# A state-space scan and a dilated local attention on one core: q·k products laid out by head dimension, and the scan as a tree in PSUM

## The chip, the core and the metric

The kernel runs on one core of one Trainium2 chip. The time is the device time in microseconds (us) of one execution; of several executions the median is given. The engines of a core work beside each other and meet through semaphores: TensorE (PE, matrix products into PSUM; its weight loads are a row of their own, PEld), VectorE (DVE), ScalarE (ACT), GpSimd (POOL) and SyncE (SP), whose queue issues most of the transfers. The trace comes from one profiled execution.

## The reference

Two independent heads work on inputs of 2048 positions and 448 channels, and their outputs stand side by side in 896 columns.

Head A is a diagonal state-space model with 448 complex states. With `Lam_bar = exp(dt*Lam)` and `B_bar = ((Lam_bar-1)/Lam)*B` it computes, position after position,

```
h = Lam_bar * h + B_bar @ x[t]
y[t] = 2 * Re(C @ h) + Dskip * x[t]
```

Head B is attention with 16 heads of 28 dimensions. `q, k, v = x @ wqkv`; a position attends to itself and to the positions 2, 4, ..., 14 before it (8 taps, `w`), those before the start being masked; softmax over the taps; the weighted sum of v goes through `wo`. Inputs and output are bf16.

## The kernel before, in words

The 2048 positions are cut into 128 chunks of 16. A chunk is a partition wherever positions lie on partitions, and `j` (0 to 15) is the place in the chunk, so that a tile `[128, 16, 448]` holds a whole head's input.

**Head B.** `prep` (L197) transposes x for each j on PE (L213), copies it to SBUF (`xT`, ACT, L216) and multiplies it with Wk (`_proj_unit`, L189), chunks on the output's partitions. DVE copies k to `kd` (L219), ACT q to `qd` (L232), both as `[128 chunks, j, dim, head]`. Positions from the chunk before (a halo of 14) come by DMA within SBUF (`_halo`). `qk` (L255) takes, for each block of 8 j (`b` = 1, then 0) and each tap w, one product of 3584 elements a partition (L265), adds the upper half of the 28 dimensions to the lower (L267) and again to 7 (L270), and PE adds those 7 into PSUM with an identity as weights (L276). ACT copies the logits out (L282), POOL masks (L288). `softmax` (L299) takes maximum and sum by halving over the taps on DVE. `pv` (L328) multiplies attention weights and v and accumulates on DVE (L348, L351, L352) in three parts of 8, 6 and 2 j, with two partial sums; per j PE transposes and adds these (`pt_o`, L364), ACT copies (`oT`, L369), PE multiplies with `wo` (L374), ACT copies (`yb`, L379), SP stores (L382).

**Head A.** `setup` derives, from the parameters, the powers of Lam_bar as small arrays and from those matrices of 128x128 for each of 7 tiles (`m`) of 64 complex states (real parts on 64 partitions, imaginary on 64): Gdiag, Lmat, Mmat on POOL (L585, L615), Pmat on DVE (L615). `level1` (L682) runs over j: B_bar times x into PSUM (L712, 128 columns), plus Lmat times the state of j-1 (L720), copied out by ACT (L724) and stored to DRAM (`hs`). `level2` scans the 128 chunk ends in 7 doubling steps (L749, L754). `outputs` (L783) loads each j's states again (L793), adds the carry from the chunk before with identity and power matrices (L803, L805), copies (L809), and makes y (L821, L826), which ACT copies (L831) and SP stores (L837).

**Order.** Nothing runs in the order of the source. Every step is a `Unit` of `Planner` with an engine, an estimated cost, dependences, a priority and perhaps a buffer to acquire or release (PSUM tags mm 4, pt 2, lg 2 banks). `Planner.run` simulates the engines by the estimated costs, always starts the unit that can start first (ties by priority), and emits the instructions in that order. On the chip each engine keeps this order and waits where something isn't ready.

Of the kernel before, what the change touches and what calls it, by code (L numbers as in the profile page):

```python
# [10 lines left out]
ALU = mybir.AluOpType  # L11
f32 = mybir.dt.float32
# [16 lines left out]
NST = 7  # L29
PAD = 64  # L30
MA = 4
JB = 8
NB = T // JB
BH = JB * H
# [8 lines left out]
def act(n):  # L43
    return n / 1200.0 + 0.16


def vec(n):
    return n / 960.0 + 0.15


def vec2(n):
    return n / 1920.0 + 0.15
# [6 lines left out]
class Unit:  # L59
    __slots__ = ("eng", "cost", "fn", "deps", "prio", "acq", "rel", "lat", "end", "seq")  # L60


class Planner:

# [6 lines left out]
    def add(self, eng, cost, fn, deps=(), prio=0.0, acq=None, rel=None, lat=0.08):  # L71
        u = Unit()
        u.eng, u.cost, u.fn, u.prio, u.acq, u.rel, u.lat = eng, cost, fn, prio, acq, rel, lat
        u.deps = [d for d in deps if d is not None]
        u.end, u.seq = None, len(self.units)
        self.units.append(u)
        return u

    def run(self):
        left = list(self.units)  # L80
        clock = {}
        order = []
        while left:
            best = None
            for eng in {u.eng for u in left}:
                now = clock.get(eng, 0.0)
                pick = None
                for u in left:
                    if u.eng != eng or any(d.end is None for d in u.deps):
                        continue  # L90
                    if u.acq and not self.free[u.acq]:
                        continue
                    t = max([now] + [d.end - (d.lat if d.eng == eng != "SP" else 0.0) for d in u.deps])
                    if u.acq:
                        t = max(t, min(self.free[u.acq]))
                    key = (t, u.prio, u.seq)
                    if pick is None or key < pick[0]:
                        pick = (key, u)
                if pick and (best is None or pick[0][0] < best[0][0]):
                    best = pick  # L100
            assert best, "no unit can start"
            (t, _, _), u = best
            if u.acq:
                self.free[u.acq].remove(min(self.free[u.acq]))
            clock[u.eng] = t + u.cost
            u.end = t + u.cost + u.lat
            if u.rel:
                self.free[u.rel].append(u.end)
            left.remove(u)
            order.append((t, u))  # L110
        self.order = order
        for _, u in order:
            u.fn()


def _make_identity(nc, ident):
    n = ident.shape[0]
    nc.gpsimd.memset(ident, 0.0)
    nc.gpsimd.affine_select(
        out=ident, in_=ident, compare_op=ALU.not_equal, fill=1.0, base=0,  # L120
        pattern=[[-1, n]], channel_multiplier=1,
    )


class PartB:
    JG = (3, 2, 1, 0)
    PV = ((1, 8, 16, "xin"), (0, 0, 6, "qd"), (0, 6, 8, "lg"))

    def __init__(self, tc, B_x, B_wqkv, B_wo, out_b, ident, pool, psum, plan):
        self.tc, self.nc = tc, tc.nc  # L130
        self.B_x, self.B_wqkv, self.B_wo, self.out_b = B_x, B_wqkv, B_wo, out_b
        self.ident, self.pool, self.psum, self.plan = ident, pool, psum, plan

    def loads(self):
        nc, pool, P = self.nc, self.pool, self.plan
        self.x_sb = pool.tile([NCH, T, D], bf16, name="xb_sb", tag="xin")
        xv = self.B_x[0].rearrange("(p j) d -> p j d", j=T)
        self.wn = pool.tile([KP, KT, 3, H, DH], bf16, name="wqkv_nat", tag="wp")
# [3 lines left out]
        def xload(g):  # L142
            nc.sync.dma_start(self.x_sb[:, 4 * g:4 * g + 4], xv[:, 4 * g:4 * g + 4])

        def wload(w):
            nc.sync.dma_start(self.wn[:, :, w].rearrange("p k h d -> p k (h d)"), wv[w])
        for i, g in enumerate(self.JG):
            self.u_x[g] = P.add("SP", dma(458752), lambda g=g: xload(g), lat=2.5)
            w = {0: 1, 2: 0, 3: 2}.get(i)
            if w is not None:  # L150
                self.u_w[w] = P.add("SP", dma(401408), lambda w=w: wload(w), lat=2.5)
# [11 lines left out]
    def alloc(self):  # L163
        nc, pool, V = self.nc, self.pool, self.nc.vector
        self.qd = pool.tile([NCH, T, DH, H], bf16, name="qd", tag="qd")
        self.kd = pool.tile([NCH, TJ, DH, H], bf16, name="kd", tag="kd")
        self.vx = pool.tile([NCH, TJ * DH * H], bf16, name="vd", tag="vd")
        self.vd = self.vx[:].rearrange("p (j d h) -> p j d h", d=DH, h=H)
        self.xT = self.vx[0:KP, 0:T * KT * NCH].rearrange("p (g k j c) -> p g k j c", g=4, k=KT, j=4)
        self.zsrc = pool.tile([1, DH * H], bf16, name="zsrc")  # L170
        V.memset(self.zsrc[:], 0.0)

    def _zero(self, t_):
        self.nc.sync.dma_start(t_[0:1, 0:HALO].rearrange("o j d h -> o j (d h)"),
                               self.zsrc[:].unsqueeze(1).to_broadcast([1, HALO, DH * H]))

    def _halo(self, t_, i0, i1):
        nc = self.nc
        nc.sync.dma_start(t_[1:113, i0:i1], t_[0:112, i0 + T:i1 + T])
        nc.sync.dma_start(t_[113:128, i0:i1], t_[112:127, i0 + T:i1 + T])  # L180

    def _proj_unit(self, j, which, prio, deps, evict, eng, extra=()):
        nc, P = self.nc, self.plan
        box = {}

        def mm():
            ps = self.psum.tile([NCH, H, DH], f32, name="qkv_ps", tag="mm")
            for k in range(KT):
                nc.tensor.matmul(ps[:].rearrange("p h d -> p (h d)"), lhsT=self.xT[:, j // 4, k, j % 4, :],  # L189
                                 rhs=self.wn[:, k, which].rearrange("p h d -> p (h d)"),  # L190
                                 start=(k == 0), stop=(k == KT - 1))
            box["ps"] = ps[:].rearrange("p h d -> p d h")
        u = P.add("PE", pe(4, 448), mm, [self.u_xe[j], self.u_w[which], *deps], prio, acq="mm")
        e = P.add(eng, act(448), lambda: evict(box["ps"]), [u, *extra], prio, rel="mm")
        return u, e

    def prep(self):  # L197
        nc, P, V = self.nc, self.plan, self.nc.vector
        self.u_xe, self.u_k, self.u_kh, self.u_q = {}, {}, {}, {}
        self.u_proj = []  # L200
        self.lg, self.u_lg, self.u_d, self.u_attn = {}, {}, {}, {}
        self.attn = None
        P.add("SP", 0.1, lambda: self._zero(self.kd), prio=0)
        for g in self.JG:
            if g == 1:
                self.q_proj(1, 0)
            for j in range(4 * g + 3, 4 * g - 1, -1):
                box = {}
# [724 lines left out]
```

## Time and profile before

| | us |
|---|---|
| median of three executions | 183.8 |
| lowest, highest | 182.88, 183.84 |
| span of the profiled execution, first to last instruction | 180.6 |
| PE, DVE, ACT, POOL busy | 161.8, 157.2, 114.5, 26.8 |
| first DVE operation on data, end of the last | 8.2, 172.7 |
| first matmul | 4.73 |

The page gives no time for the profiled execution but its span; what lies around it is the rest of an execution's time, which is here taken from the median, 183.8 − 180.6 = 3.2 us. In a row of groups the columns are: line, engine, operation, output and inputs by name, shapes, how many, then busy us, mean ns of one, and idle time before them with what ended it. In an order of time: start, duration, engine, line, operation. In the chain: start, duration, what. A matmul's duration holds a latency that the next one overlaps, so PE's pace is read from the chain. In the stretch view: stretch, its length, busy time of PE, PEld, DVE, ACT, POOL, then the granted clock (1.00 is full), DMA's share, GB/s.

### The profile page before, as it was taken

How to read it: one execution, taken by the hardware profiler on the slowest of the kernel's cores; microseconds unless marked ns; L12 is line 12 of the kernel's file. 1: busy time of each engine (PE TensorE's matmuls, PEld its weight loads, DVE VectorE, ACT ScalarE, POOL GpSimd, SP SyncE). 2: the span in 40 equal slices, each digit the busy share in tenths (PEclk: the TensorE clock that was granted, in tenths of full speed). 3: DMA queues.
4: the chain of work that ended last, by engine and by line, in shares of the span. 5: the costliest groups of instructions: out<-in, count | busy, mean ns of one | idle time of the engine just before them, and what ended most of it. 6: DMA issues, size and time to landing. Idle time of an engine off the chain costs nothing.

```text
span 180.6 us, 4508 instructions
## 1 busy us (share of the span) xinstructions
PE 161.8 (90%) x1840; PEld 121.1 (67%) x1840; DVE 157.2 (87%) x175; ACT 114.5 (63%) x227; POOL 26.8 (15%) x39
## 2 busy tenths in 40 slices
PE   0889999098999999998999998989999899999992
PEld 0556567054689999964999984566777667667760
DVE  0187999999999999999999987999999999999920
ACT  2358767205788735699574358986666578756863
POOL 2000599996000000001000010000000000000000
PEclk9999999969999999999999999999999999999999
DMA  6999633637771112211454223155544323351322
GB/s 168 342 269 210 151 101 98 206 83 244 129 129 61 33 58 92 88 59 31 126 160 126 89 67 95 51 157 162 169 155 152 105 73 104 104 156 54 95 85 76
DMA packets 24643, 22.20 MB, mean 123 GB/s; under 512 B 9243, under 2 KB 23093, under 8 KB 24623
## 3 DMA queue, kind: packets, MB, share of 16 engines
q1 hardware_dynamic: 24552, 21.91, 43.8%
q8 instruction: 14, 0.23, 0.6%
q14 instruction: 6, 0.05, 0.1%
q10 hardware_dynamic: 71, 0.01, 0.0%
HBM read 11.36 MB, written 7.34 MB: 104 GB/s over the span
## 4 chain that ended last, share of the span: by engine, by line
DVE 44%; PE 38%; issue 11%; DMA 2%; ACT 2%; POOL 0%; POOLq 0%; DVEq 0%; ACTq 0%
DVE prod L265 11%; PE qkv_ps L189 9%; DVE prod L267 7%; PE wo_ps L374 7%; DVE pv_tmp L351 7%; DVE acc L352 6%; PE y_ps L826 5%; DVE s L270 5%; PE pt_o L364 4%; DMA xb_sb<-in_B_x_dram 2%; PE l1A L712 2%; PE pt_x L213 2%; DVE kd L219 2%; PE l1B L712 1%; DVE logits L310 1%
## 5 line engine op out<-in xcount | busy, mean ns | idle before, releaser
L189 PE MATMUL qkv_ps<-wqkv_nat,vd 112*128 112x448 bf16 x192 | 43.5, 369 | 1.0 <-ACT vd L216 0.5
L265 DVE TENSOR_TENSOR prod<-qd,kd 128x3584 bf16<-128x3584 bf16 x16 | 33.5, 2096 | 0.4
L189 PEld LDWEIGHTS <-vd 112*128 112x128 bf16 x192 | 18.4, 101 | 16.0 <-issue 3.0
L712 PEld LDWEIGHTS <-Bcat 112*128 112x128 bf16 x448 | 26.3, 98 | 0.0
L352 DVE TENSOR_TENSOR acc<-acc,pv_tmp 128x3584 bf16<-128x3584 bf16 (+2 forms) x18 | 25.3, 1403 | 0.6
L351 DVE TENSOR_TENSOR pv_tmp<-attn,vd 128x3584 bf16<-128x3584 bf16 (+2 forms) x18 | 25.2, 1400 | 0.5
L826 PE MATMUL y_ps<-Ccat,ht 128*128 128x448 bf16 x112 | 24.8, 352 | 0.4 <-ACT ht L809 0.2
L267 DVE TENSOR_TENSOR prod<-prod 128x1792 bf16<-128x1792 bf16 x16 | 20.2, 1263 | 0.5
L615 POOL TENSOR_TENSOR Mmat<-Dm,Scat 128x896 bf16<-128x896 f32 x7 | 17.2, 2490 | 0.0
L712 PE MATMUL l1A<-xaT_sb,Bcat 112*128 112x128 bf16 x256 | 16.9, 219 | 0.0
L219 DVE CAST kd<-qkv_ps 128x448 bf16<-128x448 f32 x16 | 9.3, 614 | 7.2 <-PE qkv_ps L189 7.2
L276 PE MATMUL lg_ps<-s,ident 128*128 128x128 bf16 x112 | 8.8, 218 | 6.8 <-DVE s L270 6.7
L826 PEld LDWEIGHTS <-ht 128*128 128x128 bf16 x112 | 9.8, 97 | 7.3 <-ACT ht L809 0.7
L831 ACT CAST ya<-y_ps 128x448 bf16<-128x448 f32 x16 | 8.5, 532 | 9.1 <-PE y_ps L826 6.6
L720 PEld LDWEIGHTS <-Lmat 128*128 128x128 bf16 x210 | 13.4, 97 | 1.3 <-issue 0.5
L270 DVE TENSOR_TENSOR s<-prod 128x896 bf16<-128x896 bf16 x16 | 12.7, 796 | 1.4
L374 PE MATMUL wo_ps<-wo_p,oT_sb 112*128 112x448 bf16 x64 | 13.4, 352 | 0.0
L276 PEld LDWEIGHTS <-ident 128*128 128x128 bf16 x112 | 7.4, 97 | 8.8 <-issue 8.0
L216 ACT COPY vd<-pt_x 112x512 bf16<-112x512 bf16 x16 | 8.7, 591 | 7.1 <-PE pt_x L213 7.1
L712 PE MATMUL l1B<-xaT_sb,Bcat 112*128 112x128 bf16 x192 | 13.0, 219 | 0.0
L379 ACT CAST yb<-wo_ps 128x448 bf16<-128x448 f32 x16 | 8.5, 532 | 6.9 <-PE wo_ps L374 6.8
L724 ACT CAST ht<-l1A 128x512 bf16<-128x512 f32 x15 | 8.8, 587 | 6.5 <-PE l1A L720 6.2
(135 smaller groups left out, 291.0 us busy)
## 6 DMA issues: line engine op xcount, KB each, us to landing
hin<-hs SPq DMA_DIRECT2D x16, 224.0 KB, 2.8
hs<-ht SPq DMA_DIRECT2D x15, 128.0 KB, 1.7
xb_sb<-in_B_x_dram SPq DMA_DIRECT2D x4, 448.0 KB, 5.4
xa_sb<-in_A_x_dram SPq DMA_DIRECT2D x2, 896.0 KB, 5.7
out_dram<-ya SPq DMA_DIRECT2D x16, 112.0 KB, 1.7
out_dram<-yb SPq DMA_DIRECT2D x16, 112.0 KB, 1.7
hs<-ht SPq DMA_DIRECT2D x15, 96.0 KB, 1.6
wqkv_nat<-in_B_wqkv_dram SPq DMA_DIRECT2D x3, 392.0 KB, 4.9
```

What stands on the lines that cost most here:

```text
L189: nc.tensor.matmul(ps[:].rearrange("p h d -> p (h d)"), lhsT=self.xT[:, j // 4, k, j % 4, :], rhs=self.wn[:, k, which].rearrange("p h d -> ...
L265: V.tensor_tensor(pr[:].rearrange("p d j h -> p j d h"), self.qd[:, j0:j0 + JB], self.kd[:, o:o + JB], op=ALU.mult)
L267: V.tensor_tensor(pr[:, 0:14], pr[:, 0:14], pr[:, 14:28], op=ALU.add)
L270: V.tensor_tensor(s7[:], prf[:, 0:7], prf[:, 7:14], op=ALU.add)
L276: nc.tensor.matmul(box["lps"][:, w % 4, :], lhsT=self.ident[:], rhs=box[w][:, d, :], start=(w % 4 == 0 and d == 0), stop=(d == 6), skip_gr ...
L351: V.tensor_tensor(tmp[:], aa, vv, op=ALU.mult)
L352: V.tensor_tensor(acc[:, g], acc[:, g], tmp[:], op=ALU.add)
L374: nc.tensor.matmul(ps[:], lhsT=jb["oT"][:, kt, :], rhs=self.wo_p[:, kt, :], start=(kt == 0), stop=(kt == KT - 1))
L615: eng.tensor_tensor(out_tile, dm.unsqueeze(1).unsqueeze(1).to_broadcast([NCH, n, 2, PL]), scal.unsqueeze(3).to_broadcast([NCH, n, 2, PL]), ...
L712: nc.tensor.matmul(ps[:, m - m0, :], lhsT=self.Bcat[:, k, m, :], rhs=self.xT[:, j, k, :], start=(k == 0 and m == m0), stop=(j == 0 and k = ...
L720: nc.tensor.matmul(box[j, h][:, m - m0, :], lhsT=Lm[:, i * NM + m, :], rhs=pv[:, m, :], start=False, stop=(i == 1), skip_group_check=True)
L826: nc.tensor.matmul(jb["y"][:], lhsT=self.hts[:, j % 3, m, :], rhs=self.Ccat[:, m, :], start=False, stop=(m == NM - 1), skip_group_check=True)
```

## The change

The file is rewritten. Layouts, buffers, the planner's costs and priorities and most of both heads are new.

- q and k are projected transposed: the output's partitions are channels, in 7 column groups of 128 of the joined q and k (the columns of Wk are rotated so that the groups fill), 512 positions at a time. The chunks are put in an order (even and odd) in which "one chunk earlier" is a shift by two columns, so that k's halo is a slice; POOL copies its edge column.
- A product (DVE) takes 4 j, one tap and all channels, 2048 elements a partition; no halving adds. PE sums the 28 dimensions of each head with 0/1 selectors of 32 columns into 32 PSUM partitions for each j, 256 columns a matmul. The mask is a matmul that opens the accumulation.
- The logits stay in PSUM; maximum by one reduction (DVE), subtraction and sum by matmuls, exp (ACT) out of PSUM, normalization on DVE, transposed back on PE.
- V, pv and wo stay as they are in kind; pv runs in two parts of 8 j with one sum.
- Head A's scan takes one tile of 64 states after the other. A tile's 2048 positions lie in two double PSUM banks; pairs, then groups of 4, 8 and 12, then the chunks (radix 4) are combined in place by matmuls with power matrices, and the carries run back down the same tree. Nothing goes to DRAM. The power matrices are built on DVE from bf16 pairs, three tiles ahead; Gdiag is on DVE too.
- Many PSUM copies may go to ACT or DVE; the planner picks the one that starts first, until a time limit. PSUM tags: P 1 and Q 2 double banks, s 2 single banks. SBUF regions are shared by hand.

```diff
+    def evict(self, n, fn, deps, prio, rel=None, acq=None, until=None):
+        if until is None:
+            return self.plan.add("ACT", act(n), lambda: fn("ACT"), deps, prio, acq=acq, rel=rel)
+        return self.plan.add(("ACT", "DVE"), (act(n), vec(n)), fn, deps, prio, acq=acq, rel=rel, until=until)
...
-                pr = pool.tile([NCH, DH, JB, H], bf16, name="prod", tag="prod")
-                V.tensor_tensor(pr[:].rearrange("p d j h -> p j d h"), self.qd[:, j0:j0 + JB],
-                                self.kd[:, o:o + JB], op=ALU.mult)
-                V.tensor_tensor(pr[:, 0:14], pr[:, 0:14], pr[:, 14:28], op=ALU.add)
...
-                V.tensor_tensor(s7[:], prf[:, 0:7], prf[:, 7:14], op=ALU.add)
...
-                    nc.tensor.matmul(box["lps"][:, w % 4, :], lhsT=self.ident[:], rhs=box[w][:, d, :],
-                                     start=(w % 4 == 0 and d == 0), stop=(d == 6), skip_group_check=True)
...
+                    pr = ub["pr"] = pool.tile([NCH, 2, KT, 4, NCH], bf16, name="prod", tag="PR", bufs=3)
...
+                            V.tensor_tensor(pr[:, i, :, n:4], self.qT[:, :, j0 + n:j0 + 4, :],
+                                            self.kT[:, :, o:o + 4 - n, 2:QW], op=ALU.mult)
...
+                            V.tensor_tensor(pr[:, i, :, 0:n], self.qT[:, :, j0:j0 + n, :],
+                                            self.kT[:, :, o:o + n, 0:NCH], op=ALU.mult)
...
+                    for kt in range(KT):
+                        for i in range(4):
+                            nc.tensor.matmul(lg[32 * i:32 * i + 32, 2 * tp:2 * tp + 2, :],
+                                             lhsT=cx.Z[:, kt, H - H * par:3 * H - H * par],
+                                             rhs=pr[:, :, kt, i, :],
+                                             start=False, stop=(kt == KT - 1), skip_group_check=True)
...
+                u = P.add("PE", pe(16, 64) + 0.2 + (pe(2, 512) if first else 0), summ, [u] + sums[:1], -2, rel="PR",
...
+            V.tensor_reduce(box["mx"][:], self.lg[b][:].rearrange("p w q -> p q w"), axis=AX.X, op=ALU.max)
...
+    def powers(self, m, prio, deps):
...
+            V.tensor_tensor(t[:], self.o["Dm"][:].rearrange("p (a b) -> p a b", b=2).unsqueeze(1).to_broadcast(
...
+            a = P.add("PE", pe(4, 512), lambda f=bproj: f("P", 0, True), dx + prev2, pr, acq="P")
+            a = P.add("PE", pe(4, 512), lambda f=bproj: f("P", 2, False), [a], pr)
+            eP = P.add("ACT", act(1024), evP, [a] + prev2, pc, rel=None if keep else "P")
+            late = qk_done if m >= NHO else []
+            q = P.add("PE", pe(4, 512), lambda f=bproj: f("Q", 1, True), dx + [a] + late, pr, acq="Q")
+            q = P.add("PE", pe(4, 512), lambda f=bproj: f("Q", 3, False), [q], pr)
+            u = P.add("PE", pe(2, 512), s1, [eP, q], pc)
+            u = P.add("ACT", act(512), ev1, [u], pc)
+            u = P.add("PE", pe(1, 512), s2, [u], pc)
+            u = P.add("ACT", act(384), evG, [u], pc)
+            u = P.add("PE", pe(1, 768), s3, [u], pc)
+            for n, (unit, ks) in enumerate(((1, (1, 2, 3)), (4, (1, 2, 3)), (16, (1, 2, 3)), (64, (1,)))):
+                u = P.add("ACT", act(128), lambda f=evv, n=n: f(n % 2), [u], pc)
+                u = P.add("PE", pe(len(ks), 128), lambda f=l2, n=n, unit=unit, ks=ks: f(n % 2, unit, ks), [u], pc)
+            eh = P.add("ACT", act(128), lambda f=evv: f(0), [u], pc)
+            u = P.add("PE", pe(3, 128), s4, [eh], pc)
+            u3 = P.add("ACT", act(512), ev3, [u], pc)
+            u = P.add("PE", pe(2, 256), s5, [u3], pc)
+            u1 = P.add("ACT", act(512), ev1f, [u], pc, rel="Q")
...
+            done[m] = P.add("ACT", act(1024), evPf, [u], pc, rel="P")
...
-    BUFS = {"mm": 4, "pt": 2, "lg": 2}
+    BUFS = {"P": 1, "Q": 2, "s": 2}
```

1109 lines of the change are left out of this document (607 added, 502 removed).

## The prediction, made before the changed kernel was run

> **What bounds the kernel now.** I read the page's busy shares and its chain first, then the groups with shapes kept apart, then the order of time on VectorE (DVE), ScalarE (ACT) and TensorE (PE).
>
> ```profile
> span 180.6 us, 4508 instructions
> ...
> PE 161.8 (90%) x1840; PEld 121.1 (67%) x1840; DVE 157.2 (87%) x175; ACT 114.5 (63%) x227; POOL 26.8 (15%) x39
> ...
> DVE 44%; PE 38%; issue 11%; DMA 2%; ACT 2%; POOL 0%; POOLq 0%; DVEq 0%; ACTq 0%
> ```
>
> Two engines are nearly full and share the chain, so a change must lighten both. Groups:
>
> ```profile
> L265 DVE TENSOR_TENSOR prod<-qd,kd 128x3584 bf16<-128x3584 bf16 x16 | 33.5, 2096 | 0.4
> L267 DVE TENSOR_TENSOR prod<-prod 128x1792 bf16<-128x1792 bf16 x16 | 20.2, 1263 | 0.5
> L270 DVE TENSOR_TENSOR s<-prod 128x896 bf16<-128x896 bf16 x16 | 12.7, 796 | 1.4
> L351 DVE TENSOR_TENSOR pv_tmp<-attn,vd 128x2688 bf16<-128x2688 bf16 x6 | 9.3, 1556 | 0.1
> L219 DVE CAST kd<-qkv_ps 128x448 bf16<-128x448 f32 x16 | 9.3, 614 | 7.2 <-PE qkv_ps L189 7.2
> L369 ACT CAST oT_sb<-pt_o 112x512 bf16<-112x512 f32 x16 | 8.7, 596 | 0.9 <-PE pt_o L364 0.9
> ```
>
> Products and their two halving adds are 66.4 of DVE's 157.2 us. The order of time shows that some of this is delay:
>
> ```profile
> 28.71 2.79 DVE L265 TENSOR_TENSOR prod<-qd,kd 128x3584 bf16<-128x3584 bf16 x1
> 31.53 2.46 DVE L267 TENSOR_TENSOR prod<-prod 128x1792 bf16<-128x1792 bf16 x1
> 34.02 1.99 DVE L270 TENSOR_TENSOR s<-prod 128x896 bf16<-128x896 bf16 x1
> ...
> 44.95 2.01 DVE L265 TENSOR_TENSOR prod<-qd,kd 128x3584 bf16<-128x3584 bf16 x1
> 46.99 1.09 DVE L267 TENSOR_TENSOR prod<-prod 128x1792 bf16<-128x1792 bf16 x1
> 48.12 0.62 DVE L270 TENSOR_TENSOR s<-prod 128x896 bf16<-128x896 bf16 x1
> ```
>
> Until 43.5 us POOL builds matrices out of SBUF (L615, seven of 2.49 us) and DVE's operations run up to three times as long; two sets lose 6.6 us. From the chain comes PE's pace:
>
> ```profile
> 145.82 0.90 PE pt_o L364 x16
> ...
> 147.28 1.52 PE wo_ps L374 x8
> ```
>
> That is 56 ns for 128 columns and 189 for 448, so 0.42 ns a column and 216 for 512. Two more lines, of the stretch view and of the waits:
>
> ```profile
> 8.20:172.70 164.50, 153.56 (x1784) 116.20 (x1784) 156.81 (x172) 107.57 (x215) 25.59 (x20) 0.99 0.44 119
> ```
>
> ```profile
> PE lg_ps L276 <- DVE s L270: 6.7, 7, 4.5
> ```
>
> DVE (third pair) works 156.8 of the 164.5 us between its first operation on data and its last: 7.7 us of gaps, 7.9 before, 7.9 of tail.
>
> **DVE, part by part.** Removed: products and adds, 66.4. Added: 32 products of 2048. Same operation and type as L267 and L351: 1.09 at 1792 and 1.56 at 2688 give 1.22, and 0.03 between starts, 1.25; four are cut in two by the chunk edge (0.19 each): 40.8. Softmax now costs 12.6 (max and sum trees, subtraction, reciprocal, product); left are a reduction (1.23, as L310 at 1024), reciprocal (0.95) and product (1.23), twice: 6.9. pv loses its split: 30 operations of 2.04, 61.2 instead of 58.8. L219 (9.3) and Pmat (5.2) go. Seven power builds of 1920 bf16 cost 1.16 at the paired rate, 8.2, but 2.19 each at Pmat's unpaired rate (1.08 at 896), 7 more; I take the first, the types being those of L351. Gdiag comes from POOL: 1.1. Setup loses some 0.6. The 6.6 us of delay are in the 66.4, and what stays on POOL is mostly memsets: its 0.85 us memset at 82.59 lies inside a product of the usual 2.0.
>
> The unknown is E, the evictions that the planner gives to ACT or DVE, whichever starts first. By L219 and L369 all cost 54.8 us on DVE (32 of the projections 30.4, Bcat 4.8, A's x 9.8, V 9.8) or 46.9 on ACT. ACT's own work is 79.5 (scan 39.6 from seven tiles of 5.65; oT, yb, ya 25.3; the rest 14.6), about 31 of it in the first 75 us where these also fall: 78 in 70, so E is at least 10. Above that DVE is the busier; I take 20, bounds 10 and 30. B's xT is now written with every second element skipped, which no row shows: free by L244's reordered read (0.545 against 0.532 for yb), at most doubled, which would put 8 us more on ACT's share; I take free.
>
> Sum: 157.2 − 66.4 + 40.8 − 12.6 + 6.9 − 58.8 + 61.2 − 9.3 − 5.2 + 8.2 + 1.1 − 0.6 + 20 = 142.5. Start 7.9 and gaps 7.7 I leave; cover for the early gaps are the evictions. The tail grows: block 0's eight columns j all wait for its last add, where now two do (DVE ends at 172.7). Each holds a bank of tag s for about 1.0 us (pt_o 0.22 with its latency 0.22, oT 0.60) and one for 1.5 (wo_ps 0.9, yb 0.53); two banks: 1.25 a column, 10.0, then the store (177.97 to the end, 2.6) and hops: 12.9. ACT alone would need 9.1. Span by DVE: 7.9 + 142.5 + 7.7 + 12.9 = 171.0.
>
> **PE.** Passes now by the pace: qkv 36.3, L712 25.2, L720 11.8, corrections 12.6, level 2 with ga 4.0, y 24.4, wo 12.1, pt_o 7.2, logit sums 6.3, transposes and weights 11.7: 151.6, so 29.0 uncovered. After: q and k in 112 passes of 512, 24.2 as before; V 12.1; scan seven times 6.26 (16 projection passes 3.46, ten carry products and the copy back 2.80), 43.8; y 24.4; wo 12.1; pt_o 3.6; masks and softmax 3.6; the rest 11.7: 135.5. To it come 256 selector matmuls of 256 columns with 32 output partitions. No row shows such a shape. If four at different partition blocks run together: 27 ns; one after another: 110. Their weights (32 of the 128 columns that load in 97 ns) add 24 ns each where hidden by nothing, which makes (97 + 110)/4 = 52 for four together. I take 45, nearest that: 11.5, ends 7 and 28.
>
> [...]
>
> Of PE's 29.0 uncovered, 6.7 and 0.9 wait for DVE; 21.4 stay. The first projection now needs Wq too, 0.4 MB more at 261 GB/s: 1.5; the tail leaves PE 1.7 idle. 135.5 + 11.5 + 24.6 = 171.6, so PE ends beside DVE.
>
> **Moved work and waits.** hs goes (15 double stores, 16 loads, ~3.7 MB written), kd's halo goes, A's x is loaded in four quarters behind B's transposes; SP issues fewer (0.3 to 0.8 us each), and DMA is busy 44%: nothing on the path; without that cover each quarter of A's x would cost up to the 5.7 us that a load takes to land. POOL gets four 16-element copies in the halo's place and a one-partition memset of V's first rows, which only pv's third step needs; by the row above neither delays DVE. The builds of powers 3 to 6 wait on DVE for an earlier scan tile, with prods and pv queued behind them; cover: three buffers. A scan tile is 11 round trips between PE and ACT:
>
> ```profile
> 99.96 0.48 ACT L724 CAST ht<-l1B 128x384 bf16<-128x384 f32 x1 [0.63 <-PE l1B L720]
> 101.06 0.48 ACT L724 CAST ht<-l1B 128x384 bf16<-128x384 f32 x1 [0.63 <-PE l1B L720]
> ```
>
> 1.10 a trip, less 0.48 and six passes, leaves 0.28 of hand-off. ACT 5.65, PE 2.15, hand-offs 3.1: 10.9 us a tile. Three tiles run under the products on the one Q bank left (from about 40 us), four more two at a time after the last exp at about 98: 98 + 22 = 120, y 24.4 and block 1's pt_o and wo 7.9: 152, before pv ends at 158. Hidden.
>
> The median of the runs, 183.8, stands 3.2 over the profiled span, and I add that: 171.0 + 3.2 = 174.2.
>
> **Rivals.**
> (1) Selectors one after another. For: no row shows overlap. Against: only the shape. PE 135.5 + 28.1 + 24.6 = 188.2, time 191.4, slower. It decides from 80 ns a matmul (135.5 + 24.6 + 20.5 = 180.6).
> (2) The array empties at each change between 32-wide and 128-wide passes: 16 groups, 32 changes, 0.16 us each (L276: 218 ns against a pace of 56): PE 171.6 + 5.2 = 176.8, time 180.0. [...]
> (3) The scan's trips take what level 2's took: L754's evictions start every 1.78 us where 1.10 would be clean, 1.62 times: 17.7 a tile. 98 + 35.4 + 24.4 + 7.9, then block 0's 7.9 and 3.3: 176.9, time 180.1. From 19.5 a tile it reaches today's span. For: the scan shares PE and ACT. Against: under pv both are nearly free.
> (4) E near 10 and gaps of 4: 157.3, time 160.5. For: evictions can fill waits. Against: PE's sum.
>
> **How the numbers follow.** DVE sets the end as summed: 0.45 (168 to 181 alone, from E and the power builds). (1) 0.18, (2) 0.10, (3) 0.14, (4) 0.13. The time is the first's, 174.2; 163 to 190 leaves out about half of (4) and the upper half of (1), 0.17. A difference under 0.5% (the three runs span 0.5%) can't be told from none. Faster: 0.42 + 0.01 + 0.07 + 0.08 + 0.13 = 0.71; same: 0.06; slower: 0.02 + 0.16 + 0.01 + 0.04 = 0.23.
>
> **What would show it.** prod 2048 at 1.22 us with no long ones early; DVE near 142 busy; E as DVE's share of the casts; selectors' start-to-start distance, 27, 52 or 110 ns; DVE waiting for PE before casts and power builds would speak for (1) or (2); y still running when pv ends, for (3). Wrong it would be if the paired rate failed on products (39 us more) or if DVE's in-order queue waits for a PE that is late against the plan.

## The result, and the profile after

The changed kernel takes 176.9 us (median of 4 runs, 176.2 to 177.2) where the kernel before takes 183.8 on the same chip (4 runs, 182.9 to 183.9): a ratio of 0.963, 95% interval 0.960 to 0.966. The forecast was 174.2, with a range of 163 to 190. The profiled execution took 176.2 us, with a span of 174.5. The page of after, its span, busy shares and chain by engine:

```profile
span 174.5 us, 3174 instructions
...
PE 154.7 (89%) x1284; PEld 86.7 (50%) x1284; DVE 129.1 (74%) x130; ACT 107.0 (61%) x188; POOL 18.8 (11%) x47
...
PE 43%; DVE 38%; ACT 9%; issue 6%; DMA 2%; ACTq 0%; DVEq 0%
```

DVE lost 28.1 us of work (157.2 to 129.1) and the span only 6.1, so most of that gain went somewhere. The groups of after, with shapes kept apart (busy us and mean ns of one behind the bar):

```profile
L391 DVE TENSOR_TENSOR prod<-qk 128x2048 bf16<-128x2048 bf16 x16 | 18.8, 1217 | 3.6 <-ACT qk L157 3.6
L404 PE MATMUL logits<-prod,Zsel 128*32 128x256 bf16 x256 | 9.9, 275 | 0.0
L832 DVE TENSOR_TENSOR pw<-Dm,spair 128x1920 bf16<-128x1920 bf16 x7 | 7.9, 1152 | 0.0
L161 DVE COPY rb<-pt_x 112x1024 bf16<-112x1024 bf16 x4 | 5.1, 1290 | 8.3 <-PE pt_x L322 8.3
L157 ACT COPY xaT_sb<-pt_xa 112x1024 bf16<-112x1024 bf16 x5 | 5.0, 1028 | 1.4 <-PE pt_xa L819 1.3
```

Products (1.22 us at 2048 elements) and power builds (1.15 at 1920) take 0.60 ns an element, where L267 and L351 of the kernel before take 0.61 and 0.58 outside the delays, as priced. The selectors' 275 ns is one matmul's latency; their pace is in the chain:

```profile
29.52 0.55 PE logits L404 x16
```

Sixteen take 0.55 us, 34 ns each, where 256 columns at the pace of the 128-wide passes are 110 ns: in the trace the four at different output partitions start within 0.010 us (29.452 to 29.462) and the next four 0.12 us behind them (29.571), so four overlap. The order of time (start, duration, engine, line; in brackets the idle time ahead and what ended it) around the two places where DVE and TensorE meet:

```profile
120.07 2.02 DVE L528 TENSOR_TENSOR rb<-rb,pv_tmp 128x3584 bf16<-128x3584 bf16 x1
122.15 0.65 PE L542 MATMUL pt_o<-unperm,rb 128*112 128x128 bf16 x8 [0.55 <-DVE rb L528]
...
137.18 0.36 PE L986 MATMUL y_ps<-Dg,xaT_sb 112*128 112x112 bf16 x4
...
149.96 2.02 DVE L528 TENSOR_TENSOR rb<-rb,pv_tmp 128x3584 bf16<-128x3584 bf16 x1
152.04 0.65 PE L542 MATMUL pt_o<-unperm,rb 128*112 128x128 bf16 x8 [0.23 <-DVE rb L528]
```

Block 1's pt_o waits at 122.15 for the last add of pv. The last scan tile ends at 137.6 and y, 24.4 us of passes, starts at 137.2, when only 14.8 us are left until pv ends; seven of its sixteen groups stand behind block 0's pt_o. From 137.2 to its last wo pass at 170.6 TensorE's only pause is the 0.23 us ahead of this pt_o.

Summed by TensorE, with passes counted at their pace as in the prediction: they fell from 151.6 to 144.3 (the 135.5 of the sum, and 256 selectors at 34 ns, 8.8). What is left of the span, the time not covered by passes, went from 29.0 to 30.2; it is a remainder, so the two make up the 6.1 us by themselves and prove nothing. DVE's saving stands as idle time: 16.1 us of gaps and 22.5 us behind its last operation, where the prediction had 7.7 and 12.9.

### The profile page after: what moved, and what is told of

Its sections match the earlier page's. It is cut to its first block, busy times and chain, and to the rows that moved or that the text cites. A ratio compares the mean times of both kernels' runs of the same rounds, so it can differ in the third digit from the quotient of the medians.

```text
span 174.5 us, 3174 instructions
## 1 busy us (share of the span) xinstructions
PE 154.7 (89%) x1284; PEld 86.7 (50%) x1284; DVE 129.1 (74%) x130; ACT 107.0 (61%) x188; POOL 18.8 (11%) x47
## 4 chain that ended last, share of the span: by engine, by line
PE 43%; DVE 38%; ACT 9%; issue 6%; DMA 2%; ACTq 0%; DVEq 0%
DVE pv_tmp L527 16%; DVE rb L528 12%; PE qk_ps L292 10%; PE v_ps L476 6%; PE y_ps L989 5%; PE logits L404 4%; PE wo_ps L552 3%; ACT qk L157 2%; DMA ra<-in_B_x_dram 2%; DVE rb L524 2%; DVE rb L161 2%; ACT rb L157 2%; PE scQ L873 2%; PE scP L873 2%; DVE pw L832 2%
## 5 line engine op out<-in xcount | busy, mean ns | idle before, releaser
L292 PE MATMUL qk_ps<-rb 112*128 112x512 bf16 x112 | 27.8, 397 | 2.3 <-DVE rb L161 1.0
L528 DVE TENSOR_TENSOR rb<-rb,pv_tmp 128x3584 bf16<-128x3584 bf16 x14 | 28.3, 2025 | 0.5
L527 DVE TENSOR_TENSOR pv_tmp<-attn,vd 128x3584 bf16<-128x3584 bf16 x14 | 28.2, 2018 | 0.0
L391 DVE TENSOR_TENSOR prod<-qk 128x2048 bf16<-128x2048 bf16 (+1 forms) x20 | 21.2, 1110 | 3.6 <-ACT qk L157 3.6
L395 DVE TENSOR_TENSOR prod<-qk 128x2048 bf16<-128x2048 bf16 (+1 forms) x16 | 16.7, 1084 | 0.2 <-PE logits L404 0.2
L873 PEld LDWEIGHTS <-Bcat 112*128 112x128 bf16 x112 | 10.4, 97 | 11.9 <-issue 2.7
L873 PE MATMUL scP<-xaT_sb,Bcat 112*128 112x512 bf16 x56 | 13.9, 378 | 2.1 <-ACT late L940 1.3
L989 PE MATMUL y_ps<-Ccat,late 128*128 128x448 bf16 x64 | 14.7, 352 | 0.0
L552 PE MATMUL wo_ps<-wo_p,rb 112*128 112x448 bf16 x64 | 14.0, 352 | 0.3 <-ACT rb L547 0.3
L476 PE MATMUL v_ps<-rb 112*128 112x448 bf16 x64 | 14.2, 353 | 0.0
L873 PE MATMUL scQ<-xaT_sb,Bcat 112*128 112x512 bf16 x56 | 13.6, 379 | 0.0
L995 ACT CAST late<-y_ps 128x896 bf16<-128x896 f32 x8 | 7.2, 905 | 10.2 <-PE y_ps L989 9.4
L157 ACT CAST qk<-qk_ps 128x1024 bf16<-128x1024 f32 (+2 forms) x10 | 7.6, 756 | 8.5 <-PE qk_ps L292 6.0
L161 DVE COPY rb<-pt_x 112x1024 bf16<-112x1024 bf16 x4 | 5.1, 1290 | 8.3 <-PE pt_x L322 8.3
L157 ACT CAST vd<-v_ps 128x448 bf16<-128x448 f32 x13 | 6.8, 537 | 5.5 <-PE v_ps L476 5.4
```

What stands on the lines that cost most here:

```text
L157: nc.scalar.copy(out, in_)
L292: nc.tensor.matmul(box["ps"][:, i], lhsT=lhs(k), rhs=self.xT[:, 4 * g:4 * g + 4, k, :], start=(k == 0), stop=(k == KT - 1), skip_group_che ...
L391: V.tensor_tensor(pr[:, i, :, n:4], self.qT[:, :, j0 + n:j0 + 4, :], self.kT[:, :, o:o + 4 - n, 2:QW], op=ALU.mult)
L395: V.tensor_tensor(pr[:, i, :, 0:n], self.qT[:, :, j0:j0 + n, :], self.kT[:, :, o:o + n, 0:NCH], op=ALU.mult)
L527: V.tensor_tensor(tmp[:], aa, vv, op=ALU.mult)
L528: V.tensor_tensor(self.acc[:, b], self.acc[:, b], tmp[:], op=ALU.add)
```

## Experiments: which chain sets the end

Theory A is the prediction's: DVE sets the end. B: two chains meet, DVE with pv, and the scan with wo and y on TensorE. C: the scan alone. D: TensorE alone. All times are medians, to be held against 176.9; every ratio is against the kernel before in the same batch. That kernel gave 182.7 to 183.8 in the five batches, so a difference of about 1 us from 176.9 can't be told from none.

**Two taps less on DVE.** In `pv`, the written order kept:

```
             def step(w=w, o=o):
                 alloc()
+                if b == 0 and w >= 6:
+                    return
```

> The changed kernel without taps 6 and 7 of block 0 in pv (their products and adds are left out, so block 0's output lacks two of eight taps); the written order of everything else is kept. DVE has four operations of 2.02 us less, 8.1 us, all of them just before its last one, so pv should end near 144 in place of 152.0. Theory A, DVE sets the end (the prediction's sum): 8 us less, span near 166.5. Theory B, two chains end together - DVE's pv, and the scan with the y passes behind it, which keep TensorE full from 137.2 - so that shortening one alone gives nothing: 0 to 1 us less, TensorE's passes still at the same times after 137. Theory C, the scan alone sets the end: the same 0 here.

Measured: 176.6 (ratio 0.963, 0.958 to 0.968). Pv ended at 144.2, 7.8 us sooner, and nothing followed. A is out for this stretch.

**Four round trips less in each scan tile.**

```
-            def evv(dst, box=box, pb=pb):
+            def evv(dst, box=box, pb=pb, last=False):
+                if not last:
+                    return
...
             def l2(src, unit, ks, box=box, pb=pb, L=L):
+                return
...
-            eh = P.add("ACT", act(128), lambda f=evv: f(0), [u], pc)
+            eh = P.add("ACT", act(128), lambda f=evv: f(0, last=True), [u], pc)
```

> The changed kernel without the four radix-4 steps over chunks in each scan tile (28 of 35 copies L902 and the 91 matmuls L907 and L912 are left out, so A's scan stops at the chunk edge; the copy that the carry needs stays); the written order is kept. Each tile loses four of eleven round trips of about 1.0 us; with two tiles in flight the last tile should complete 8 to 14 us earlier than 137.6. Theory A, DVE sets the end: 0. Theory B, two chains end together: y starts earlier, but block 0's pt_o stands behind nine of the sixteen y groups and waits for pv at 152, and seven y groups and four pairs of wo follow it as before: 0 to 1 us less, with TensorE idle just before 152. Theory C, the scan alone sets the end: 8 to 12 us less.

Measured: 175.9 (0.958, 0.952 to 0.964), 1.0 less, where C expected 8 to 12. But this alone doesn't rule C out, since the last tile didn't end sooner: y started at 137.50. (0.9 us of that is a later start of this execution, which is shown two runs below.) The reason is in the order of time of this run:

```profile
117.45 1.89 PE L873 MATMUL scP<-xaT_sb,Bcat 112*128 112x512 bf16 x8 [1.10 <-ACT late L943]
121.54 0.65 PE L542 MATMUL pt_o<-unperm,rb 128*112 128x128 bf16 x8 [2.20 <-DVE rb L528]
122.03 2.70 PE L873 MATMUL scQ<-xaT_sb,Bcat 112*128 112x512 bf16 x8
```

Block 1's pt_o stands in TensorE's order ahead of the sixth tile's second half, and it waits 2.20 us for DVE. And the same eight passes that took 1.89 us before this wait take 2.70 behind it; that is the next section's matter.

**Both at once.**

> Both edits at once: pv of block 0 without taps 6 and 7, and the scan without its radix-4 steps (both computations left out). Theory A: 8 us less, as with the taps alone. Theory C: 8 to 12 less, as with the radix steps alone. Theory B, two chains end together: only now does the end move, by 7 to 9 us, to a span near 166.5, though each edit alone gave nothing.

Measured: 175.5 (0.956, 0.950 to 0.962), 1.4 less where B expected 7 to 9. So B was wrong on where the chains meet: not at 152 but, if it holds, at 122. In this run too pt_o came at 121.39, after 2.20 us of waiting for block 1's pv, which the taps left out of block 0 can't shorten, and y at 137.34.

**Taps out of block 1 in place of block 0, with the scan shortened.** This tests the meeting at 122 (the condition in `step` is `b == 1`, the rest as in the second run).

> The changed kernel without the radix-4 steps of the scan (as in the second experiment) and without taps 6 and 7 of block 1 in pv (in place of block 0; both computations left out), the written order kept. So block 1's pv ends at 114 instead of 122 and block 0's near 144. Theory A, DVE sets the end: 8 us less than the changed kernel's 176.9. Theory B as the runs so far leave it: DVE and the scan meet at 122, where block 1's pt_o waits for its last add behind the scan's passes in TensorE's order, and from there to 170.6 TensorE is full. With the radix steps gone the passes ahead of pt_o ended at 119.4, so pt_o should now start there, 2.7 us earlier, and everything behind it too; with 1.1 us of passes less behind it and no idle time over 1.2 us, so no half clock: 3 to 4.5 us less. Theory C, the scan alone: as with the radix steps alone, 0 to 1 less.

Measured: 171.1 (0.935, 0.928 to 0.942), 5.8 less, and 5.1 by the spans (169.4 against 174.5):

```profile
118.25 0.61 PE L544 MATMUL pt_o<-unperm,rb 128*112 128x128 bf16 x8
...
132.48 0.36 PE L991 MATMUL y_ps<-Dg,xaT_sb 112*128 112x112 bf16 x4
```

Pt_o no longer waits and starts 3.9 us sooner than in the changed kernel, y 4.7 sooner, the span is 5.1 shorter. The same taps that gave nothing in block 0 are worth 4.4 us more in block 1 (171.1 against 175.5), and only DVE's work differs between these two runs, so D, TensorE alone, is out. B holds, with the meeting at 122. Block 1's taps without the radix edit were not tried; in the changed kernel pt_o waits only 0.55 us, so they could free little more than that there.

The gain is above the 3 to 4.5 expected, which had been reckoned from the run without radix steps, and there every pass from 14 us on is 0.9 us later than here. That is the start of the execution. The first sixteen projection passes took 6.32 us in that run, 5.42 in this one and 5.31 in the changed kernel, where sixteen at full pace take 3.46. The trace's record of the clock begins, at full, at 13.74, 11.90 and 11.77 us (the stretch view writes 1.00 where there is no record yet), and half of 13.74 − 11.90 is 0.92. In the traces of the changed kernel and of the variants that keep its order this point lies between 11.8 and 13.9 us, so up to 1.0 us of a single execution's time is decided there.

**Pv made longer.**

```
                     V.tensor_tensor(tmp[:], aa, vv, op=ALU.mult)
+                    if b == 0 and w >= 4:
+                        V.tensor_tensor(tmp[:], aa, vv, op=ALU.mult)
```

> The changed kernel with pv's products of taps 4 to 7 of block 0 made twice (the second writes the same numbers over the first; nothing is left out), the written order kept: four operations of 2.02 us, 8.1 us more on DVE, all between 134 and 152, so that pv ends near 160. Theory A, DVE sets the end: 8 us more. Theory B, two chains meet (DVE with pv, and TensorE with scan, wo and y, each at its limit): taking 8 us off DVE gave nothing, but adding 8 costs nearly all of it, 7 to 8 us, since the nine y groups ahead of block 0's pt_o are done at 152. Theory C, DVE has room: 0 to 2.

Measured: 187.8 (1.026, 1.021 to 1.030): 10.9 more, for 8.1 us of work, where B expected 7 to 8. Less work gave nothing and more costs more than all of it; the next section shows where the rest comes from.

**A new order for a lighter DVE, and for a shorter scan.** Here the units are left out of the plan itself, so the planner writes a new order: pv without taps 6 and 7 of both blocks, then the scan without radix steps.

```
-        for w in range(W):
+        for w in range(W - 2 if b in (0, 1) else W):
```

> The changed kernel without taps 6 and 7 in both blocks of pv (the output lacks two of eight taps), with the order of the whole program worked out anew by the kernel's own planner. DVE has eight operations of 2.02 us, 16.2 us, less. If DVE is the engine that sets the pace (the prediction's sum): 12 to 16 us less. If TensorE's passes and the scan's trips set it, and DVE only meets them where the order was fitted to it: 0 to 2 us, either way.

Measured: 178.2 (0.974, 0.968 to 0.981). 16.2 us of DVE's work taken away, DVE done at 137, and the kernel is no faster; nor are the two executions that ran at full clock throughout (177.3 and 177.4). DVE's work as summed doesn't set this kernel's pace.

```
-            for n, (unit, ks) in enumerate(((1, (1, 2, 3)), (4, (1, 2, 3)), (16, (1, 2, 3)), (64, (1,)))):
+            for n, (unit, ks) in enumerate(()):
```

> The changed kernel without the four radix-4 steps in each scan tile (A's scan stops at the chunk edge), with the order worked out anew by the kernel's planner. TensorE has 3.7 to 4.8 us of passes less (70 and some matmuls of 128 columns at 56 ns), ACT 7.6 us of copies, and each tile four of eleven round trips. If DVE sets the pace: 0 to 1 us less. If the scan and TensorE behind it do: 4 to 8 us less, the last tile done some 8 to 13 us sooner than 137.6 and y starting with it. With the old order the same edit gave 0.9 us, since the passes after it stayed where they had been written.

Measured: 174.0 (0.950, 0.945 to 0.954), 2.9 less, below the 4 to 8 expected, though y started at 127.5, 9.7 us sooner. So C, the scan alone, is out. 1.7 us of what is missing went in the way that the next section shows.

**Wide selectors.** The sums' price: each selector padded to 128 columns, so that each matmul writes all 128 output partitions.

```
-        Z = self.Z = pool.tile([NCH, KT, 3 * H], bf16, name="Zsel")
+        Z = self.Z = pool.tile([NCH, KT, 240], bf16, name="Zsel")
...
-                            nc.tensor.matmul(lg[32 * i:32 * i + 32, 2 * tp:2 * tp + 2, :],
-                                             lhsT=cx.Z[:, kt, H - H * par:3 * H - H * par],
+                            nc.tensor.matmul(lg[:, 2 * tp:2 * tp + 2, :],
+                                             lhsT=cx.Z[:, kt, 112 - 32 * i - H * par:240 - 32 * i - H * par],
```

> The changed kernel with each selector padded with zeros to 128 columns, so that each of the 256 selector matmuls writes all 128 output partitions and nothing can run beside it; same result, same written order. By TensorE's pace a matmul of 256 columns is 110 ns against the 34 ns of a 32-wide one in the chain: 256 x 76 ns = 19.5 us more of passes, groups of 16 at 1.75 us in place of 0.55. Rival 1 of the prediction gave 191.4 for a kernel in which the selectors run one after another. If TensorE's passes bound the kernel in the middle (it idles 0.5 us or less in each 10 us from 50 to 90): 12 to 19 us slower, some 189 to 196. If the products on DVE hide the longer sums (a product pair takes 2.5 us, a group of sums 1.75): 0 to 6 us slower.

Measured: 193.2 (1.053, 1.047 to 1.058), 16.3 more. Sixteen take 1.75 us in this run's chain, 109 ns each, against 0.55. By the groups:

```profile
L404 PE MATMUL logits<-prod,Zsel 128*128 128x256 bf16 x256 | 30.5, 273 | 0.0
```

The mean is that of the 32-wide ones (275), which shows that it is latency and not pace. So rival 1's mechanism was priced well (191.4) and did not occur. The run also says which engine bounds the middle: 16.3 of the 19.5 us of passes added there came through to the end.

## Experiments: the granted clock, and where the gain came from

**The skip term left out.**

```
-                for k in range(KT):
-                    nc.tensor.matmul(ps[:, k * KP:(k + 1) * KP], lhsT=self.xT[:, j + jj, k, :], rhs=self.Dg[:, k, :],
-                                     start=(k == 0), stop=False, skip_group_check=True)
```

> The changed kernel without the 64 skip-term matmuls L986 in y (A's output lacks x times D), the written order kept: 0.19 us less in each of sixteen y groups, 3.0 us of TensorE passes, all after 137.2. Nine groups stand ahead of block 0's pt_o, which waits for DVE at 152.0; seven stand behind. Theory A, DVE alone: 0. Theory B: 7 x 0.19 = 1.3 us less (the nine ahead only wait longer at 152). Theory D, TensorE alone sets the end: 3.0 less.

Measured: 177.3 (0.961, 0.952 to 0.971). 3.0 us of passes less made nothing faster; in the median neither B's 1.3 nor D's 3.0 came. The stretch view of this run, with TensorE's busy time first and the granted clock third from the right:

```profile
151.10:153.00 1.90, 0.00 (x0) 0.00 (x1) 1.84 (x1) 0.00 (x0) 0.00 (x0) 1.00 0.37 125
153.90:157.10 3.20, 3.20 (x10) 1.32 (x9) 0.00 (x0) 1.54 (x3) 0.00 (x0) 0.50 0.00 0
157.30:170.00 12.70, 12.70 (x86) 7.29 (x85) 0.00 (x0) 7.97 (x14) 0.00 (x0) 1.00 0.33 108
```

TensorE idles for 1.9 us, and then works at half clock for 3.4 us, which costs 1.7. Three of the four executions had a mean clock of 0.985 to 0.987 and took 177.2 to 178.0; the fourth had 0.997 and took 174.7, 2.2 less than the changed kernel, between B's 1.3 and D's 3.0.

**The wait filled with work.** In the kernel with the longer pv:

```
+                for _ in range(6 if (j, jj) == (8, 0) else 1):
                     for k in range(KT):
                         nc.tensor.matmul(ps[:, k * KP:(k + 1) * KP], lhsT=self.xT[:, j + jj, k, :], rhs=self.Dg[:, k, :],
                                          start=(k == 0), stop=False, skip_group_check=True)
...
```

> The kernel with the longer pv (the products of taps 4 to 7 of block 0 made twice), and in addition the ninth y group, the last one ahead of block 0's pt_o, made six times over, each time from the start of its accumulation (the same numbers; nothing is left out): 5 x 1.525 = 7.6 us more of TensorE passes, in the 8.9 us for which TensorE waited idle there. If the granted clock of 0.5 that the profile shows from 156 to 166 us in that run comes from the idle time, the clock stays at 1.0 here and the kernel gets faster by more work: the 5.4 us at half clock after the wait cost 2.7, so 2 to 3 us less than 187.8. If it does not come from the idle time: 0, or up to 1 us more.

Measured: 185.1 (1.009, 1.006 to 1.012), 2.8 less than without the filler. The stretches of the run with the wait, then of the run with the filler:

```profile
152.20:161.00 8.80, 0.39 (x4) 0.40 (x5) 8.25 (x5) 0.00 (x0) 0.00 (x0) 0.72 0.08 27
161.00:166.30 5.30, 5.30 (x23) 2.69 (x22) 0.00 (x0) 2.06 (x4) 0.00 (x0) 0.50 0.00 0
```

```profile
152.00:161.00 9.00, 8.27 (x59) 4.51 (x57) 8.90 (x5) 0.11 (x1) 0.00 (x0) 1.00 0.08 26
161.00:166.30 5.30, 5.18 (x41) 3.19 (x42) 0.06 (x1) 2.94 (x5) 0.00 (x0) 1.00 0.19 63
```

With TensorE kept busy the clock stays at 1.00, and 7.6 us more of matmuls make the kernel faster. So it is TensorE's idle time that halves the clock. What is left over 176.9 is 8.2 us, pv's 8.1.

Half clock came after idle time in seven of these runs: behind 1.9 us in the run without the skip term, behind 2.2 us (and 1.1 shortly before) in the runs without radix steps, behind 1.24, 0.41 and 0.63 within 3 us in the one with the new order. It lasts 3.4 us or two or three times that (6.8, 10.2).

What decides is where the wait falls. The traces record every change of the clock, and in all fourteen traces the changes stand a whole number of 3.413 us behind the first (8 in the kernel before, from 9.43 to 36.74, 32 without radix steps, 41 without the skip term). Cut the time at these points. Of the 665 stretches of 3.413 us at full clock, TensorE was busy for 47% or less in 22 (14 of them at the kernels' ends), and half clock followed every one; in the other 643 it was busy for 48% or more, and it followed none. Full clock came back only behind stretches that were 95% busy or more; behind 69% and 77% it did not. In the run without the skip term, the stretch from 150.38 to 153.79 holds 1.48 us of matmuls, 43%. By this a wait of about 2 us costs another 1.7 where it falls into one stretch, as it did there, and should cost nothing where two stretches share it. That may be why the fourth execution above escaped; only a slower one was traced, so this isn't shown.

**POOL in the kernel before.** The kernel before has such a stretch too, which the prediction did not look at:

```profile
36.06 0.55 PE L276 MATMUL lg_ps<-s,ident 128*128 128x128 bf16 x7 [4.52 <-DVE s L270]
```

```profile
31.50:36.06 4.56, 0.05 (x1) 0.00 (x0) 4.50 (x3) 1.01 (x3) 4.56 (x3) 1.00 0.66 209
36.70:40.10 3.40, 3.40 (x17) 1.97 (x16) 3.37 (x3) 0.00 (x0) 3.40 (x2) 0.51 0.35 89
```

TensorE waited 4.5 us for DVE's first products, which were long while POOL built matrices (2.79, 2.46 and 1.99 us), and then ran 3.4 us at half clock. So in the kernel before (its eight builds of scan matrices become memsets, of which the seven of Mmat are shown):

```
-            self._build(G, self.Mmat[:, s_ * NM:(s_ + 1) * NM], o["Dm"][:], self.Scat[:, 6 + s_], NM)
+            for _ in range(3):
+                G.memset(self.Mmat[:, s_ * NM:(s_ + 1) * NM], 0.0)
```

> The kernel before, with POOL's builds of Lmat and Mmat (L615, reads and writes of SBUF) replaced by three memsets each of the same tiles (writes alone, of about the same total time: 0.85 us for 896 elements; the scan's matrices are zeros, so A's output is left out). If it was POOL's operations, whatever their kind, that made DVE's early products up to three times as long (2.79, 2.46 and 1.99 us in place of 2.04, 1.09 and 0.62), the early groups stay at their long durations. If it was POOL reading SBUF beside DVE: they come down to 2.04, 1.09 and 0.62, DVE's busy time falls by 6 to 7 us, and the time by 0 to 5 us (TensorE is nearly as full).

Measured: 177.0 (0.965, 0.959 to 0.970), 6.8 less than the kernel before, above the 0 to 5 expected. The groups and the same stretch of this run:

```profile
L265 DVE TENSOR_TENSOR prod<-qd,kd 128x3584 bf16<-128x3584 bf16 x16 | 32.3, 2022 | 0.4
L267 DVE TENSOR_TENSOR prod<-prod 128x1792 bf16<-128x1792 bf16 x16 | 17.5, 1092 | 0.6
L270 DVE TENSOR_TENSOR s<-prod 128x896 bf16<-128x896 bf16 x16 | 10.0, 625 | 1.4
```

```profile
36.70:40.10 3.40, 3.40 (x24) 1.90 (x23) 3.33 (x6) 2.39 (x5) 3.29 (x5) 1.00 0.80 241
```

POOL is as busy as before, with memsets, and every product runs at its usual time; DVE's busy time is 150.5 in place of 157.2. TensorE's waits for these sums fell from 6.7 to 1.8 us, and the half clock is gone. So it was the builds, which read SBUF, and not POOL's being busy; which part of a build does it, no run takes apart. This edit alone, which leaves out the builds, is worth 6.8 us, and the whole rewrite, which moves them to DVE (9.0 us there), 6.9.

**A version that shortens both chains.** It computes all of it; the edits to the scan, the power buffers and y are shown, the planner's priorities and costs and the loads of B's x changed too:

```
-            for n, (unit, ks) in enumerate(((1, (1, 2, 3)), (4, (1, 2, 3)), (16, (1, 2, 3)), (64, (1,)))):
+            for n, (unit, ks) in enumerate(((1, (1, 2, 3, 4, 5)), (6, (1, 2, 3, 4, 5)), (36, (1, 2, 3)))):
...
-            t = pool.tile([NCH, 2 * NPW, 32, 2], bf16, name="pw", tag="pw", bufs=3)
+            t = pool.tile([NCH, 2 * NPW, 32, 2], bf16, name="pw", tag="pw", bufs=4)
...
+            hd = self.u_h[:-3] if n < 2 else self.u_h
+            u = P.add("PE", pe(6, 448) + pe(4, 112), lambda f=y: f(0), hd + self.u_cc + [self.u_dg], pr, acq=tag)
+            u = P.add("PE", pe(6, 448) + pe(4, 112), lambda f=y: f(1), [u], pr)
+            u = P.add("PE", pe(2, 448), yl, [u] + self.u_h, pr)
```

> A version that computes all of it and shortens both chains and the clock's cause together, as the runs so far ask for. The scan over chunks goes in three steps (1 to 5, 6 to 30, 36 to 108 chunks) in place of four: one round trip of about 1.0 us less in each tile, three matmuls of 128 columns and three powers more. Power tables have four buffers in place of three, so that DVE can build them earlier than in pv's stretch. The last tile's term of y becomes a matmul of its own, so that the first two pairs of y can start without it. B's x is loaded in eighths. The planner gets the measured durations (1.31 us for the permuted copy, 0.71 for the bf16 copy on DVE, 0.55 for sixteen selectors), and its priorities are chosen so that TensorE is never idle for 1.85 us in any 3 us. By the planner's own count the last eviction ends 4 us sooner than in the changed kernel's order. Theory B (two chains that meet, and a clock that halves after idle time): 2 to 6 us less than the changed kernel's 176.9, 171 to 175, with the clock at 1.0. Theory A, DVE alone: DVE has no work less and 1.4 us more, 0 to 1 us slower than the changed kernel.

Measured: 175.8 (174.5 to 177.9; 0.960, 0.954 to 0.966), 1.1 less where 2 to 6 were expected, which can't be told from the changed kernel: no version that computes everything is shown to beat it. Its profile has the reason, at the other end of the kernel:

```profile
24.20:26.50 2.30, 0.01 (x1) 0.00 (x0) 2.30 (x3) 1.29 (x1) 0.00 (x0) 0.83 0.45 118
26.50:32.60 6.10, 6.09 (x34) 3.98 (x34) 4.73 (x4) 2.94 (x3) 0.00 (x0) 0.50 0.08 32
```

A wait of 2.30 us for the copy of B's transposes on DVE, and twice 3.4 us at half clock behind it, which cost 3.1. The order was chosen so that TensorE should never idle for 1.85 us in any 3 us; on the chip it did. The executions with a mean clock of 0.995 to 0.997 took 174.5 to 174.9, the others 176.8 to 177.9.

## Why the prediction was right, and where its steps were wrong

The sign, the range and nearly the size were right (174.2 against 176.9), by another way than the one named. That the size came so near is luck: DVE's sum was 13.4 us too high, and the scan, held to be hidden, ended 17.6 us late.

- **"Both engines share the chain, so a change must lighten both"** fell. In the kernel before, the memsets on POOL took 6.7 us off DVE and no pass off TensorE, and gave 6.8: TensorE had been waiting for DVE at one place. In the rewrite TensorE's passes fell by 7.3 us and DVE's work by 28.1, and the span by 6.1.
- **"DVE sets the end as summed"** fell. Busy 129.1, not 142.5. Of the 13.4, 8 are E, the evictions on DVE: their groups add up to 11.9 (20 taken, lower end 10). That is one half of rival 4's condition; the other, gaps of 4, did not come: they were 16.1. Products (37.9 against 40.8), powers (7.9 against 8.2) and softmax were priced well. (The "32 of the projections 30.4" within E's price on DVE doesn't follow from L219, whose 0.61 us at 448 columns make some 22; the total on ACT, 46.9, is near the 47.9 that all these copies took on both engines, and E was taken by ACT's side.) But a lighter DVE brought nothing, as the run without sixteen microseconds of pv shows; rival 4's 160.5 was a sum for the wrong engine.
- **"Before pv ends at 158. Hidden." is the step that failed.** The scan was to be done at 120 and y by 152. It was done at 137.6, and y and wo ran 18 us beyond pv. The third tile, to be done under the products by 98, ended at 102.6. From the second tile's end (92.6) to the last's five tiles took 9.0 us each with two in flight, 18 us a tile and not 10.9. Three causes are seen: the 3.5 us of the tile's own projection passes, which the sum left out; the one pair of P banks, which both tiles share; and block 1's pt_o, which waits for DVE at 122 and stands ahead of the sixth tile's second half in TensorE's order. The size and the sign are rival 3's (17.7 a tile, "y still running when pv ends", 180.1); its cause, trips made slow by others on the same engines, is only part of it: four trips of eleven left out gave 1.0 us in the same order and 2.9 in a new one, and the wait at 122, taken away on top of them, 4.4.
- **The tail of 12.9** was 22.5, for the same reason: y groups stand between block 0's columns.
- **TensorE's sum** came nearest: 171.6 predicted, 174.5 measured, with passes 2.7 lower (selectors at 34 ns, not 45) and 5.6 more uncovered, two misses of opposite sign. The prediction treated the two engines as a tie at 171; what decided was TensorE's written order, with its wait for DVE at 122 in the midst of it.
- **Rivals 1 and 2:** the first did not occur; one after another the selectors cost 16.3 us more. Of the second a part did. In all 16 groups of after the first selector comes 0.09 us late (behind a 512-column pass 0.309 us after its start, where the pace is 0.215) and the pass behind the last four 0.10 late (0.213 in place of 0.109): 3.2 us for the 32 changes, where 5.2 were priced. The trace shows the late starts alone; that the array empties there was the author's supposition. The lower end of 7 us for all 256 is an estimate from four that run together, 27 ns each; 8.8 were measured, with the 0.10 behind each group.
- **"Free" for the permuted copy of B's x:** 1.29 us on DVE and 1.31 on ACT, where plain ones of the same size take 0.69 and 1.03: 4 x 0.60 and 4 x 0.28, 3.5 us in all. It was not off the path either: the page's chain runs through these copies (DVE rb L161 2% of the span, ACT rb L157 2%).
- **The 6.6 us of delay by POOL** were seen and counted on DVE, and TensorE's waits for these sums (6.7 us) were taken off its uncovered time. What was passed over is that POOL's builds made most of these waits (1.8 us are left with memsets in their place), and that the longest, 4.5 us, brought 3.4 us at half clock behind it. The granted clock of 0.99 over the long stretch, shown in the prediction, was this.

What stays open: how much each of the three causes of the slow scan takes (only the wait at 122 was taken away), and whether the rewrite with POOL's builds out of the account, that is products, selectors and scan against the old form, brings anything: the builds were left out and not moved in the run with the kernel before.

## What to carry to other kernels

Two engines near 90% don't say which of them to lighten: 6.7 us off DVE gave 6.8 in the kernel before, and 8 to 16 us off DVE gave nothing in the changed one. What counts is the place where the two meet: look in the order of time for the instruction of one that waits for the other, if only a few tenths, and cut what lies before it; where both chains arrive together, both have to be shortened there. Read the row of the granted clock for every dip, also when its mean is 0.99, and look for the wait ahead of it: here waits of TensorE of 1.9 to 2.3 us cost another 1.7 to 3.1 behind them, so a cut that leaves such a wait can gain nothing, and a wait removed can gain more than its length. And before a rewrite, try the one suspected nuisance by itself: here memsets in place of POOL's builds gave as much as the rewrite, though they leave the builds out.

## What the runs showed of the hardware that was not expected

- TensorE's clock changed only at points a whole number of 3.413 us apart, and it was halved behind each such stretch in which TensorE was busy for 47% or less (22 of 22) and behind none of 48% or more (643). 1.9 us of idle time were enough, and one execution of four of the same kernel kept its clock. Extra matmuls in the wait kept it at 1.00 and saved 2.8 us.
- The first passes of an execution ran at half pace, until 11.8 to 13.9 us in the changed kernel and the variants that keep its order, although the program's start is the same in all: 5.3 to 6.4 us for the first sixteen projection passes, where full pace is 3.5. In the changed kernel passes of 512 columns start 0.43 us apart before 11.77 and 0.215 behind it.
- 128x32 selector matmuls of 256 columns at 34 ns each, four starting within 0.010 us, in the midst of 128-wide passes, against 109 ns for 128-wide ones one after another; each change of width costs 0.09 to 0.10 us.
- A copy of 1024 bf16 elements out of PSUM on DVE takes 0.69 us, as long as 512 f32 (0.69); with every second element skipped on writing 1.29.
- DVE's product and its two adds took 2.79, 2.46 and 1.99 us beside POOL's builds, which read SBUF, against 2.01, 1.09 and 0.62 later in the same run, and 2.02, 1.09 and 0.63 on average with memsets on POOL in the builds' place.
